# Fused attention and Fourier mixing with a feed-forward network: weight sums formed in the first feed-forward block, feed-forward PSUM split by accumulator, block sums on GpSimd

## The chip, the cores and the metric

The kernel runs on one core of one Trainium2 chip. The metric is the device time of one execution in microseconds. The core has a matrix engine (TensorE, PE in the profile, with PEld for its weight loads), two elementwise engines that can read the matrix engine's accumulators (VectorE or DVE, ScalarE or ACT), a general engine that can't (GpSimd or POOL), and SyncE (SP), which here only issues DMAs. Each engine works through its own instructions strictly in the order that was fixed at build time; between engines, semaphores make an instruction wait for its data or for a buffer to come free. PSUM, the accumulator memory, has eight banks of 512 floats per partition.

## The reference, cut to what matters

```python
# q, k, v: (8, 12, 448, 64); w_pre, w_post: (12, 12)
scores = scale * np.matmul(q, k.transpose(0, 1, 3, 2))
scores = np.einsum('bhij,hg->bgij', scores, w_pre)
attn = softmax(scores)                       # max, exp, sum + 1e-9
attn = np.einsum('bhij,hg->bgij', attn, w_post)
x = np.matmul(attn, v) -> (8, 448, 768)

u = x + np.real(fft(fft(x, axis=1), axis=2))
un = (u - mean(u)) / np.sqrt(var(u) + 1e-06)
out = u + np.maximum(un @ w_ch1, 0.0) @ w_ch2   # (768, 3072), (3072, 768)
```

`w_ch1` and `w_ch2` come as 64-bit floats, everything else as 32-bit floats. The kernel computes in 32-bit floats.

## The kernel before, in words

**The mixing stage** (`mix_phase`) makes `u` and writes it to a scratch in device memory. The scores of ten query rows and all twelve heads stand as one tile of 120 rows. There are 360 such tiles; a loop at the end of the function takes one step for each, and in each step it emits one tile's gather (a DMA on SyncE, L248), pre-mix matmul (L254), row maximum (L261, VectorE), exponential (L270, ScalarE), reciprocal (L278 and L280, VectorE), scaling of the post-mix matrix (L283, GpSimd), flip matmul (L291) and copy out of PSUM. What is not done for every tile (loading and transposing q and k, L161 and L222; scores, L234; the products with v, L315; the Fourier steps, L345 and L369) lies in a list `fill` with due steps, and is emitted in order of those. The tile framework then orders the instructions of each engine by its own estimate of when they can run, within what the buffers allow; so an entry of the list may run well ahead of its step.

The weight conversion is such an entry too (`emit_convert`). There are 96 pieces of 128 x 384, 48 of each matrix, due every 3.5 steps. A piece is loaded as pairs of 32-bit words by a GpSimd DMA (L399, tag `raw64`, two buffers) and made into floats by seven VectorE instructions (L414 to L427). The feed-forward network multiplies 2 x 2 blocks of matrices by Strassen's scheme in Winograd's form, with seven products in place of eight. This needs four weight blocks and some sums of them. Four pieces, one of each block, fill slots of one buffer `wu` (pool `pwu`, one buffer); after the fourth, four GpSimd sums (L431) are formed in it, and the seven operands are stored by SyncE to the scratches `w1s` (L532, three DMAs) or `w2s` (L543).

**The feed-forward stage** (`ffn_phase`) takes 512 rows of `u` at a time, in 7 blocks. `norm` normalises 128 rows and transposes them into `ub`, and after the fourth forms the four input sums (L627). `first` multiplies by the first matrix: for each of six pairs of tiles `m` it runs the seven products in the order 0, 1, 4, 5, 2, 6, 3 for both tiles, in three accumulators for each tile. Accumulator P takes products 0, 5, 6 and 3 and is read out after each; Q takes 1; R takes 4 and 2. The read-outs are L651, L655, L657 (ScalarE copies), L653, L659, L661 (VectorE additions) and L663. The weights of one `m` are one DMA of seven operands (L589, three buffers). `second` multiplies by the second matrix in the same way, with its weights loaded by half an operand (L594, four buffers), and adds to `u` (L696). The normalising of the next block runs inside it. All accumulators and the transposes of `norm` take PSUM tiles of one tag with eight buffers (`ps_tile`).

Of the kernel before, what the change touches and what calls it, by code (L numbers as in the profile page):

```python
# [10 lines left out]
F32 = mybir.dt.float32  # L11
# [5 lines left out]
P = 128  # L17
# [104 lines left out]
def mix_phase(ctx, tc, ident, q, k, v, w_pre, w_post, u_scr, weights):  # L122
# [7 lines left out]

    praw = pool("praw", 2)
    pqt = pool("pqt", NHP)
# [9 lines left out]
    pcv = pool("pcv", 2)  # L142
    pwu = pool("pwu")
    cst = pool("cst")
# [249 lines left out]

    units = {}

    def emit_convert(key, slot, src, r0, c0, sums, store):
        raw = pcv.tile([P, WC, 2], U32, name="raw64", tag="raw64")
        nc.gpsimd.dma_start(  # L399
            out=raw.rearrange("p n w -> p (n w)"),  # L400
            in_=src[r0:r0 + P, c0:c0 + WC].bitcast(U32))

        def done():
            if key not in units:
                units[key] = [pwu.tile([P, 8, WC], F32, name="wu", tag="wu"), 0]
            wu = units[key][0]
            units[key][1] += 1
            lo, hi = raw[:, :, 0], raw[:, :, 1]
            top = wu[:, slot, :]
            tmp = pcv.tile([P, WC], F32, name="tmp", tag="tmp")  # L410
            topb, tmpb = top.bitcast(U32), tmp[:, :].bitcast(U32)


            nc.vector.tensor_scalar(tmpb, hi, 0x7fffffff, None, op0=ALU.bitwise_and)  # L414
# [3 lines left out]
            nc.vector.tensor_scalar(topb, tmpb, 0x07ffffff, 3, op0=ALU.bitwise_and,  # L418
                                    op1=ALU.logical_shift_left)
# [7 lines left out]
            nc.vector.tensor_tensor(top, top, tmp[:, :], op=ALU.add)  # L427
            ev.d += 7 * (60.0 + WC * 1.042)
            if units[key][1] == 4:
                for out, x, op, y in sums:  # L430
                    nc.gpsimd.tensor_tensor(wu[:, out, :], wu[:, x, :], wu[:, y, :],  # L431
                                            op=op)
                store(units.pop(key)[0])
        return 0, [done]
# [9 lines left out]
    for gn, g in enumerate(groups):  # L444
# [19 lines left out]
        if g["gi"] == NG - 1:  # L464
# [5 lines left out]
            for x in range(NG):  # L470
                due(f + n + 7.6 + x, lambda g=groups[gn - NG + 1 + x]: emit_s2(g))
    for x, cut in enumerate(weights(nc)):
        due(x * WSTEP, lambda cut=cut: emit_convert(*cut))
# [40 lines left out]


ORDER = (0, 1, 4, 5, 2, 6, 3)
# [4 lines left out]

def _pieces(nc, w_ch1, w_ch2, w1s, w2s):

    out = []

    s1 = [(4, 7, ALU.add, 3), (5, 4, ALU.subtract, 0),
          (6, 0, ALU.subtract, 7), (2, 1, ALU.subtract, 5)]
    for n in range(DFF // 2 // WC):
        for kc in range(NK):
            def store(wu, n=n, kc=kc):  # L530
                for j in range(WC // P):
                    nc.sync.dma_start(out=w1s[n * (WC // P) + j, :, :, kc, :],  # L532
                                      in_=wu[:, 0:7, j * P:(j + 1) * P])
            for i, j in ((0, 0), (0, 1), (1, 0), (1, 1)):
                slot = {(0, 0): 0, (0, 1): 1, (1, 0): 7, (1, 1): 3}[i, j]
                out.append((("w1", n, kc), slot, w_ch1, j * DH + kc * P,
                            i * (DFF // 2) + n * WC, s1, store))

    s2 = [(4, 7, ALU.subtract, 0), (5, 2, ALU.subtract, 4),
          (6, 2, ALU.subtract, 7), (3, 1, ALU.subtract, 5)]  # L540
    for kf in range(NM):
        def store(wu, kf=kf):
            nc.sync.dma_start(  # L543
                out=w2s[:, kf // NQ, :, kf % NQ, :].rearrange("m p d -> p m d"),
                in_=wu[:, 0:7, :])
        for i, j in ((0, 0), (0, 1), (1, 0), (1, 1)):
            slot = {(0, 0): 0, (0, 1): 7, (1, 0): 1, (1, 1): 2}[i, j]
            out.append((("w2", kf), slot, w_ch2, i * (DFF // 2) + kf * P,
                        j * DH, s2, store))
    return out  # L550


@with_exitstack
def ffn_phase(ctx, tc, ident, u_scr, w1s, w2s, out):

# [12 lines left out]
    pst = pool("pst", 4)  # L568
    pps = pool("pps", 8, space=bass.MemoryType.PSUM)

    NT2 = TB // P
    HT = TB // 2

    def ps_tile():
        return pps.tile([P, 512], F32, name="ps", tag="ps")

# [9 lines left out]

    def load_w1(m):
        w = pw1.tile([P, 7, NK, P], F32, name="w1t", tag="w1t")
        nc.sync.dma_start(out=w[:, :, :, :], in_=w1s[m])  # L589
        return w  # L590

    def load_w2(i, half):
        w = pw2.tile([P, NQ, DH], F32, name="w2t", tag="w2t")
        nc.sync.dma_start(out=w[:, :, :], in_=w2s[i, half])  # L594
        return w
# [4 lines left out]
    def norm(t, x):  # L600
# [15 lines left out]
        for y in range(2):  # L616
            ps = ps_tile()
            for c in range(NK):
                cc = NK * y + c
                nc.tensor.transpose(ps[:, c * P:(c + 1) * P],  # L620
                                    un[:, cc * P:(cc + 1) * P], ident[:, :])
            nc.scalar.copy(  # L622
                out=ub[:, UB[y, x // 2], :, (x % 2) * P:(x % 2 + 1) * P],
                in_=ps[:, :NK * P].rearrange("p (c n) -> p c n", n=P))
        if x == NT2 - 1:
            for o, a, b in ((4, 6, 0), (5, 2, 4), (6, 2, 6), (3, 1, 5)):
                nc.vector.tensor_tensor(ub[:, o], ub[:, a], ub[:, b], op=ALU.subtract)  # L627

    def first(t):
# [5 lines left out]
        for m0 in range(0, NM, 2):  # L635
            ms = range(m0, m0 + 2)
            w = {m: load_w1(m) for m in ms}
            ps = {}
            for i in ORDER:
                for m in ms:  # L640
                    key = {0: "P", 5: "P", 6: "P", 3: "P", 1: "Q"}.get(i, "R")
                    opens = i in (0, 1, 4)
                    if opens:
                        ps[key, m] = ps_tile()
                    p = ps[key, m][:, :HT]
# [26 lines left out]
    def second(t, h):  # L672
# [4 lines left out]
        for n, i in enumerate(ORDER):  # L677
            key = {0: "P", 5: "P", 6: "P", 3: "P", 1: "Q"}.get(i, "R")
            opens = i in (0, 1, 4)
            for half in range(2):  # L680
                w = load_w2(i, half)
                for x in range(NT2 // 2):
                    if opens and half == 0:
                        ps[key, x] = ps_tile()
                    p = ps[key, x][:, :DH]
# [35 lines left out]
def kernel(  # L721
# [17 lines left out]
    u_scr = scr.tile([B * S, DM], F32, name="u_scr")  # L739
    w1s = scr.tile([NM, P, 7, NK, P], F32, name="w1s")  # L740
    w2s = scr.tile([7, 2, P, NQ, DH], F32, name="w2s")
    mix_phase(tc, ident, q, k, v, w_pre, w_post, u_scr,
              lambda nc: _pieces(nc, moe_w_ch1, moe_w_ch2, w1s, w2s))
    ffn_phase(tc, ident, u_scr, w1s, w2s,
              out.rearrange("b s d -> (b s) d"))
# [31 lines left out]
```

## Time and profile before

| what | value |
|---|---|
| median of 3 runs | 3284.43 us (3263.74 to 3286.43) |
| the profiled execution | 3276.48 us |
| its span | 3274.6 us |
| TensorE busy | 3024.8 us (92%) |
| VectorE busy | 1147.3 us (35%) |
| ScalarE busy | 794.0 us (24%) |
| GpSimd busy | 572.9 us (17%) |
| DMA | 449.91 MB, mean 137 GB/s |

The span is what the profiler recorded of one execution; the execution's own time is 1.9 us longer. A share of busy time is an average over stages: the mixing stage ends at about 1650 us, and the feed-forward blocks take the rest. In a row of a group the columns are line, engine, operation, output and inputs, shapes and count, then the busy time and the mean ns of one, then the idle time of the engine before them with what ended it. In a row of waits they are the waiting engine and line, what it waited for, and the sum in us, the number and the longest. In a row of a table of stretches they are the stretch and its length, for each engine the busy time and the number of instructions, then the clock granted to TensorE, the DMA engines' busy share and GB/s. In a row of the timeline they are the start, the duration, the engine, the line and the operation, with the idle time before it in brackets.

### The profile page before, as it was taken

Reading aid. Unit: us, or ns where it says so; the run is one execution under the profiler, and the core shown is the slowest. Engines: PE = TensorE matmul, PEld = TensorE weight load, DVE = VectorE, ACT = ScalarE, POOL = GpSimd, SP = SyncE. Lnnn points to the kernel's source line nnn. Section 1 sums busy time; section 2 is a strip of 40 time slices with the busy share of each in tenths; the row PEclk is TensorE's granted clock in tenths of the full one; section 3 lists DMA queues with packets and bytes.
Section 4 is the critical chain, followed back from the end, with each engine's and each line's share of the span. In section 5 each row is a group of like instructions: output and inputs, shape, how many; then the busy total and the mean of one; then the engine's idle time right before and its main releaser. Section 6 shows DMA issues by size and latency. Waiting matters only on the chain.

```text
span 3274.6 us, 39030 instructions
## 1 busy us (share of the span) xinstructions
PE 3024.8 (92%) x14768; PEld 2142.8 (65%) x14768; DVE 1147.3 (35%) x2843; ACT 794.0 (24%) x1940; POOL 572.9 (17%) x937
## 2 busy tenths in 40 slices
PE   6878888888899999999999999999999999999998
PEld 3545655555666767666777676686686675776775
DVE  4655556556333333333432132132222222221220
ACT  3332342433445444444211010010010010110100
POOL 4343353453413223131200000000000000000000
PEclk8898799999999999999999999999999999999999
DMA  7565566665544444444534443434434434444422
GB/s 178 136 155 144 135 154 172 164 163 153 118 82 87 85 82 96 69 99 70 186 115 154 152 170 145 166 139 165 173 135 155 161 153 153 164 150 152 155 108 106
DMA packets 146576, 449.91 MB, mean 137 GB/s; under 512 B 14175, under 2 KB 100191, under 8 KB 123095
## 3 DMA queue, kind: packets, MB, share of 16 engines
q1 hardware_dynamic: 121847, 354.61, 37.3%
q0 software_dynamic: 24544, 92.82, 9.2%
q8 instruction: 118, 1.93, 0.2%
q14 instruction: 67, 0.55, 0.0%
HBM read 315.24 MB, written 55.05 MB: 113 GB/s over the span
## 4 chain that ended last, share of the span: by engine, by line
PE 49%; issue 29%; DMA 13%; DVE 5%; POOL 2%; ACT 1%; SPq 1%; POOLq 0%; DVEq 0%; ACTq 0%
PE ps L687 10%; PE ms L315 9%; PE ps L647 9%; PE fl L291 6%; DMA raw<-in_moe_w_ch_dram 6%; PE mx L254 5%; PE ms L369 3%; PE ms L234 3%; PE ms L345 2%; DMA w1s<-wu 2%; DMA rawk<-in_k_dram 2%; DMA out_dram<-u 1%; DMA u<-u_scr 1%; DVE nmx L261 1%; DMA w2s<-wu 1%
## 5 line engine op out<-in xcount | busy, mean ns | idle before, releaser
L647 PE MATMUL ps<-ub,w1t 128*128 128x256 f32 x3528 | 791.0, 384 | 50.8 <-DVE h L661 17.2
L647 PEld LDWEIGHTS ps<-ub,w1t 128*128 128x128 f32 x3528 | 669.6, 192 | 172.2 <-ACT h L651 30.2
L687 PE MATMUL ps<-w2t,h 128*128 128x384 f32 x2352 | 763.6, 486 | 0.0
L687 PEld LDWEIGHTS ps<-w2t,h 128*128 128x128 f32 x2352 | 445.0, 190 | 303.8
L291 PEld LDWEIGHTS fl<-kw2s,PP 120*112 120x112 f32 (+1 forms) x2880 | 350.4, 185 | 241.6 <-issue 117.2
L291 PE MATMUL fl<-kw2s,PP 120*112 120x120 f32 (+1 forms) x2880 | 392.3, 282 | 66.9 <-POOL kw2s L283 56.3
L254 PE MATMUL mx<-Kr,kw 120*120 120x448 f32 x720 | 350.7, 571 | 21.9 <-ACT PP L270 16.2
L270 ACT ACTIVATE PP<-mx,nmx 120x448 f32<-120x448 f32 x360 | 228.6, 635 | 526.9 <-DVE nmx L261 488.9
L315 PEld LDWEIGHTS ms<-vn,Pav 112*120 112x120 f32 (+1 forms) x3072 | 316.0, 182 | 21.3 <-issue 16.1
L315 PE MATMUL ms<-vn,Pav 112*120 112x64 f32 (+1 forms) x3072 | 315.4, 265 | 7.7 <-issue 6.9
L261 DVE TENSOR_REDUCE nmx<-mx 120x1 f32<-120x448 f32 x360 | 221.8, 616 | 221.9 <-PE mx L254 219.6
L283 POOL TENSOR_SCALAR kw2s<-kw2g,rcp 120x120 f32<-120x120 f32 x360 | 155.5, 432 | 691.1 <-DVE rcp L280 622.4
L707 POOL DMA_DIRECT2D out_dram<-u x7 | 5.6, 795 | 1484.7 <-DVE u L696 1484.7
L696 DVE TENSOR_TENSOR u<-u,ps 128x384 f32<-128x384 f32 x98 | 54.4, 555 | 551.9 <-PE ps L687 551.9
L104 ACT COPY Pav<-fl 112x480 f32<-112x480 f32 x310 | 177.0, 572 | 252.2 <-PE ms L315 131.9
L234 PE MATMUL ms<-kT,qT 64*120 64x448 f32 (+1 forms) x768 | 210.4, 619 | 9.3 <-DVE Sb L106 6.2
L104 ACT COPY Sb<-ms 120x448 f32<-120x448 f32 (+1 forms) x324 | 161.1, 531 | 50.9 <-PE ms L234 50.7
L653 DVE TENSOR_TENSOR h<-h,ps 128x256 f32<-128x256 f32 x84 | 35.4, 422 | 332.9 <-PE ps L647 332.9
L622 ACT COPY ub<-ps 128x384 f32<-128x384 f32 x56 | 24.0, 483 | 479.8 <-PE ps L620 479.7
L234 PEld LDWEIGHTS ms<-kT,qT 64*120 64x120 f32 (+1 forms) x768 | 57.4, 182 | 121.7 <-issue 73.8
L254 PEld LDWEIGHTS mx<-Kr,kw 120*120 120x120 f32 x720 | 109.5, 193 | 30.0 <-ACT PP L270 20.8
L278 DVE TENSOR_SCALAR rcp<-den 120x1 f32<-120x1 f32 x360 | 54.5, 152 | 211.0 <-ACT PP L270 206.0
(75 smaller groups left out, 2163.3 us busy)
## 6 DMA issues: line engine op xcount, KB each, us to landing
w1t<-w1s SPq DMA_DIRECT2D x84, 1344.0 KB
w2t<-w2s SPq DMA_DIRECT2D x98, 1152.0 KB
Kr<-Sb SPq DMA_DIRECT2D x352, 210.0 KB
raw<-in_moe_w_ch_dram POOLq DMA_DIRECT2D x96, 384.0 KB, 5.7
w1s<-wu SPq DMA_DIRECT2D x36, 448.0 KB
w2s<-wu SPq DMA_DIRECT2D x12, 1344.0 KB
rawq<-in_q_dram POOLq DMA_DIRECT2D x96, 112.0 KB, 6.0
rawk<-in_k_dram POOLq DMA_DIRECT2D x96, 112.0 KB, 5.8
```

The costliest lines, as they stand in the source:

```text
L104: self.nc.scalar.copy(out=out, in_=in_)
L234: nc.tensor.matmul(sp[:n, :S], st["qT", hp][x * D:(x + 1) * D, g["i0"]:g["i0"] + n], st["kT", hp][x * D:(x + 1) * D, :], start=True, stop= ...
L254: nc.tensor.matmul(mx[:m, :S], kw1[:m, :m], tiles[T]["Kr"][:m, :], start=True, stop=True)
L261: nc.vector.tensor_reduce(nmx[:m, :], tiles[T]["mx"][:m, :S], axis=AX.X, op=ALU.max, negate=True)
L270: nc.scalar.activation(PP[:m, :], tiles[T]["mx"][:m, :S], ACTF.Exp, bias=tiles[T]["nmx"][:m, :], accum_out=den[:m, :])
L283: nc.gpsimd.tensor_scalar(kw2s[:m, :], kw2g[:m, :], rcp[:m, :], 1.0, op0=ALU.mult, op1=ALU.mult)
L291: nc.tensor.matmul(fl[:PC, jc * KR:(jc + 1) * KR], tiles[T]["PP"][:m, jc * PC:(jc + 1) * PC], tiles[T]["kw2s"][:m, :], start=True, stop=True)
L315: nc.tensor.matmul(ps[:n, hl * D:(hl + 1) * D], g["Pav"][:, jc * NH + h, :n], st["v", h // 2][:, h % 2, jc * D:(jc + 1) * D], start=(jc == ...
L345: nc.tensor.matmul(ps[:w, :SH + 1], g["xf"][par][:n, d0:d0 + w], ts[:n, g["gi"], par, :], start=(g["gi"] == 0), stop=(g["gi"] == NG - 1))
L369: nc.tensor.matmul(ps[:n, :DH + 1], st["z", par, ch][:, i0:i0 + n], tab[:w, ch, :], start=(ch == 0), stop=(ch == len(chunks) - 1))
L647: nc.tensor.matmul(p, w[m][:, i, kc, :], ub[:, i, kc, :], start=opens and kc == 0, stop=kc == NK - 1, skip_group_check=True)
L687: nc.tensor.matmul(p, lhs[i][:, half * NQ + kf, x * P:(x + 1) * P], w[:, kf, :], start=opens and half == 0 and kf == 0, stop=half == 1 and ...
```

## The change

The mixing stage now only converts. Each piece has its own result tile `top` (two buffers) and is stored by itself, by one SyncE DMA, to new scratches `w1f` and `w2f` that hold the four blocks of each matrix. The buffer `wu`, the GpSimd sums and the stores of seven operands are gone, and the q and k loads have three buffers instead of two (`praw`).

The sums are formed in the first feed-forward block. For `t == 0`, `load_w1` loads the four blocks of an `m`, forms four sums on VectorE in the tile that TensorE will use, and stores them to `w1s`. A new function `sum_w2`, called for both tiles of each pair, does the same for one twelfth of the second matrix, in a buffer of the `pw2` pool, and stores to `w2s`. Later blocks load an `m` with four DMAs, from both scratches. `load_w2` takes blocks from `w2f` and sums from `w2s`.

The PSUM tiles have three tags: four buffers for P, two for Q (which `norm` uses too) and two for R. The input sums in `norm` go from VectorE to GpSimd.

```diff
-    praw = pool("praw", 2)
+    praw = pool("praw", 3)
...
-    pwu = pool("pwu")
...
+        top = pcv.tile([P, WC], F32, name="top", tag="top")
+        tmp = pcv.tile([P, WC], F32, name="tmp", tag="tmp")
...
-            if units[key][1] == 4:
-                for out, x, op, y in sums:
-                    nc.gpsimd.tensor_tensor(wu[:, out, :], wu[:, x, :], wu[:, y, :],
-                                            op=op)
-                store(units.pop(key)[0])
+            nc.sync.dma_start(
+                out=dst, in_=top.rearrange("p (m f) -> p m f", m=split))
...
+    def ps_tile(key):
+        return pps.tile([P, 512], F32, name="ps" + key, tag="ps" + key,
+                        bufs=4 if key == "P" else 2)
...
+    def load_w1(t, m):
         w = pw1.tile([P, 7, NK, P], F32, name="w1t", tag="w1t")
-        nc.sync.dma_start(out=w[:, :, :, :], in_=w1s[m])
+        nc.sync.dma_start(out=w[:, 0:2], in_=w1f[m, :, 0:2])
+        if t:
+            nc.sync.dma_start(out=w[:, 3], in_=w1f[m, :, 3])
+            nc.sync.dma_start(out=w[:, 2], in_=w1s[m, :, 0])
+            nc.sync.dma_start(out=w[:, 4:7], in_=w1s[m, :, 1:4])
+            return w
+        nc.sync.dma_start(out=w[:, 6], in_=w1f[m, :, 2])
+        nc.sync.dma_start(out=w[:, 3], in_=w1f[m, :, 3])
+        for o, a, op, b in ((4, 6, ALU.add, 3), (5, 4, ALU.subtract, 0),
+                            (6, 0, ALU.subtract, 6), (2, 1, ALU.subtract, 5)):
+            nc.vector.tensor_tensor(w[:, o], w[:, a], w[:, b], op=op)
+        nc.sync.dma_start(out=w1s[m, :, 0], in_=w[:, 2])
+        nc.sync.dma_start(out=w1s[m, :, 1:4], in_=w[:, 4:7])
         return w
+
+    def sum_w2(kf):
+        w = pw2.tile([P, NQ, DH], F32, name="w2t", tag="w2t")
+        at = kf // NQ, slice(None), kf % NQ
+        nc.sync.dma_start(
+            out=w[:, 0:4, :],
+            in_=w2f[:, at[0], :, at[2], :].rearrange("b p d -> p b d"))
+        for o, a, b in ((4, 1, 0), (5, 3, 4), (1, 3, 1), (2, 2, 5)):
+            nc.vector.tensor_tensor(w[:, o], w[:, a], w[:, b], op=ALU.subtract)
+        for o, n in ((1, 0), (4, 2)):
+            nc.sync.dma_start(
+                out=w2s[n:n + 2, at[0], :, at[2], :].rearrange("b p d -> p b d"),
+                in_=w[:, o:o + 2, :])
...
-            ps = ps_tile()
+            ps = ps_tile("Q")
...
-                nc.vector.tensor_tensor(ub[:, o], ub[:, a], ub[:, b], op=ALU.subtract)
+                nc.gpsimd.tensor_tensor(ub[:, o], ub[:, a], ub[:, b], op=ALU.subtract)
...
-            w = {m: load_w1(m) for m in ms}
+            w = {m: load_w1(t, m) for m in ms}
+            if t == 0:
+                for m in ms:
+                    sum_w2(m)
```

More of the change, by code (lines that the diff above doesn't have):

```diff
@@ L401, in emit_convert @@
             in_=src[r0:r0 + P, c0:c0 + WC].bitcast(U32))
+        lo, hi = raw[:, :, 0], raw[:, :, 1]
+        top = pcv.tile([P, WC], F32, name="top", tag="top")
+        tmp = pcv.tile([P, WC], F32, name="tmp", tag="tmp")
+        topb, tmpb = top[:, :].bitcast(U32), tmp[:, :].bitcast(U32)
         def done():
[L404 to L411, printed above, removed]
             nc.vector.tensor_scalar(tmpb, hi, 0x7fffffff, None, op0=ALU.bitwise_and)
```

67 lines of the change are left out of this document (29 added, 38 removed).

## The prediction, made before the changed kernel had run

> **What bounds the kernel now.** I read the page's 40 slices first, then a table of stretches cut where the picture changes.
>
> ```profile
> span 3274.6 us, 39030 instructions
> ...
> PE   6878888888899999999999999999999999999998
> ```
> ```profile
> core 0: us, PE busy (x) PEld busy (x) DVE busy (x) ACT busy (x) POOL busy (x), PEclk, DMA share, GB/s
> 30.00:835.00 805.00, 656.20 (x3654) 439.74 (x3654) 468.97 (x1273) 279.35 (x680) 332.59 (x490) 0.90 0.60 154
> 835.00:1600.00 765.00, 741.58 (x4752) 527.87 (x4752) 260.34 (x750) 350.43 (x842) 189.17 (x364) 0.98 0.45 89
> 1651.00:1769.00 118.00, 113.38 (x511) 95.97 (x510) 35.17 (x71) 18.34 (x49) 0.57 (x1) 1.00 0.33 124
> 1769.00:1878.00 109.00, 109.00 (x356) 65.18 (x355) 19.46 (x26) 3.44 (x8) 0.00 (x0) 1.00 0.44 159
> ```
>
> TensorE is the bound from 835 us to the end (741.6 of 765, and 113 of 118 in the first feed-forward block). It isn't before 835 us, where it is busy 656 of 805. That stretch is the one in which weights are converted beside the mixing. The same table for the row maxima alone (one L261 per mixing step) gives the price:
>
> ```profile
> 30.00:835.00 805.00, 97.45 (x159) 0.90 0.60 154
> 835.00:1600.00 765.00, 122.02 (x198) 0.98 0.45 89
> ```
>
> Without conversion a step takes 765/198 = 3.86 us. The 159 steps before would have taken 614 us and took 805: the conversion costs **191 us**. The groups and the waits say how.
>
> ```profile
> L431 POOL TENSOR_TENSOR wu<-wu 128x384 f32<-128x384 f32 x96 | 97.7, 1028 | 14.7 <-DVE wu L427 10.1 <-DVE rcp L278 2.8
> L427 DVE TENSOR_TENSOR wu<-wu,tmp 128x384 f32<-128x384 f32 x96 | 52.6, 554 | 0.6
> L414 DVE TENSOR_SCALAR tmp<-raw 128x384 uint32<-128x384 uint32 x96 | 39.6, 413 | 155.3 <-DMA raw<-in_moe_w_ch_dram 155.3
> ```
> ```profile
> DVE wu L418 <- DMA w1s<-wu: 68.1, 11, 9.5
> DVE wu L418 <- DMA w2s<-wu: 32.8, 9, 7.2
> PE ms L222 <- DMA rawq<-in_q_dram: 28.9, 14, 9.7
> PE ms L222 <- DMA rawk<-in_k_dram: 19.5, 11, 2.9
> PE ps L647 <- DVE h L661: 17.2, 5, 4.4
> PE ps L647 <- ACT h L651: 16.2, 35, 0.5
> PE ps L647 <- ACT h L657: 16.2, 35, 0.5
> ```
>
> VectorE runs in a fixed order. When a conversion instruction at its head waits, the row maxima and reciprocals behind it wait too, and TensorE after them. There are two such waits: 155.3 us for raw pieces (L414), and 68.1 + 32.8 = 100.9 us in 20 waits, 5.0 us each, for the one sum buffer `wu` to be stored (L418).
>
> **Mixing stage.** The seven VectorE conversions of each of 96 pieces stay. Gone are the 96 GpSimd sums (97.7 us beside other work) and the single buffer's turn every four pieces: four sums, a store, 5.0 us. In its place each piece has its own result buffer, two in rotation, and its own store. I price what is left from stretches that have no turn in them: pieces two apart, whose raw buffer is the same, starting at L414.
>
> ```profile
> 45.10 0.34 DVE L414 TENSOR_SCALAR tmp<-raw 128x384 uint32<-128x384 uint32 x1
> ...
> 64.58 0.36 DVE L414 TENSOR_SCALAR tmp<-raw 128x384 uint32<-128x384 uint32 x1 [2.87 <-DMA raw<-in_moe_w_ch_dram]
> ...
> 795.84 0.36 DVE L414 TENSOR_SCALAR tmp<-raw 128x384 uint32<-128x384 uint32 x1 [0.73 <-DMA raw<-in_moe_w_ch_dram]
> ...
> 809.19 0.36 DVE L414 TENSOR_SCALAR tmp<-raw 128x384 uint32<-128x384 uint32 x1 [2.53 <-DMA raw<-in_moe_w_ch_dram]
> ```
>
> These are the first and the last of 46 such cycles, counted through the timeline; they average 10.68 us, with 103 row maxima in all, 2.24 steps each. 48 cycles would then lose 48 x (10.68 - 2.24 x 3.86) = 98 us, so 93 us less than 191. But 96 stores now stand in SyncE's queue between the gathers, and nothing in this trace shows a second ring of two buffers beside the raw one. Its price lies between nothing (a store has the whole next piece, 5.3 us, to land) and 5.0 us per piece, as in the turn: 480 us. I take 0.25 us per piece, 24 us, near the lower end, because the turn's 5.0 us held four GpSimd sums and a store of seven blocks, and this store holds one. **Conversion: -70 us** (-93 + 24, rounded). At most all 191 go.
>
> The third raw buffer for q and k aims at the waits of L222, 48.4 us of idle TensorE. Bounds 0 and -48. Half of the batches lie before 835 us, where the price above has their waits in it, which leaves 24; and GpSimd must still issue each load. **I take -15 us.**
>
> **Feed-forward PSUM.** The two rows with 35 waits are 5 pair boundaries in 7 blocks: TensorE runs one tile's products 0, 5 and 6 in a row, each behind ScalarE's copy of the same bank.
>
> ```profile
> 1900.89 0.37 ACT L651 COPY h<-ps 128x256 f32<-128x256 f32 x1 [0.91 <-PE ps L647]
> 1901.31 1.56 PE L647 MATMUL ps<-ub,w1t 128*128 128x256 f32 x6 [0.46 <-ACT h L651]
> 1902.91 0.37 ACT L657 COPY h<-ps 128x256 f32<-128x256 f32 x1 [1.65 <-PE ps L647]
> ```
>
> With one common tag, accumulator Q of the pair's first tile comes after P of its second in the rotation, and that one waits for its weight tile. With three tags Q and R of the first tile are free, products 1 and 4 go in between, and each copy is covered by 6 matmuls or more. Bounds 0 and -32.4; **I take -25 us**, since the second tile's product 0 then comes sooner after its load. L661's 17.2 us stay: VectorE is held there by the next block's input.
>
> **Block sums on GpSimd.** Four sums of 768 columns move.
>
> ```profile
> L627 DVE TENSOR_TENSOR ub<-ub 128x768 f32<-128x768 f32 x28 | 25.6, 955 | 2.4 <-ACT ub L622 1.7
> L330 POOL TENSOR_TENSOR xe<-X 120x383 f32<-120x383 f32 x24 | 24.5, 1023 | 0.0
> L647 PE MATMUL ps<-ub,w1t 128*128 128x256 f32 x3528 | 791.0, 384 | 50.8 <-DVE h L661 17.2 <-ACT h L651 16.2 <-ACT h L657 16.2
> ```
>
> On VectorE 4 x 0.955 = 3.8 us; on GpSimd, twice L330's 1.023 for twice the columns, 8.2 us. For blocks 2 to 7 two of the seven products of the previous block still follow, about 31 us of its 109, so nothing. For the first block TensorE has products 0 and 1 before the first sum: 24 matmuls at 118 us/504, 5.6 us against 2.05; later sums come every 2 us against 2.8 per product. Zero; without cover, 4.4 us.
>
> **First block.** New there: 96 sums of 384 columns on VectorE (48 for each matrix), 96 x 0.554 = 53 us on top of 35 in 118 us: it fits. Of 24 tiles four blocks of 192 KB are read and four written.
>
> ```profile
> 1590.20 3.96 SPq L589 DMA_DIRECT2D w1t<-w1s  x3
> 1594.20 2.60 SPq L594 DMA_DIRECT2D w2t<-w2s  x4
> ```
> ```profile
> w1t<-w1s SPq DMA_DIRECT2D x84, 1344.0 KB
> ...
> raw<-in_moe_w_ch_dram POOLq DMA_DIRECT2D x96, 384.0 KB, 5.7
> ```
>
> A block is 1344/7 = 192 KB, so 24 x 8 x 196,608 B = 37.7 MB, against 14.6 (124 GB/s x 118). At full share the conversion stretch moves 154/0.60 = 257 GB/s, the first block 124/0.33 = 376, the later mixing 89/0.45 = 198: 147 us, 100 or 191. I take 147, since its rows are nearest in size. Seven of the 24 tiles can be fetched from 1590 us on, which leaves 104 in 118 us: it fits, barely. What doesn't hide is VectorE at a sum whose tile hasn't landed, with the evictions behind it. The nearest row is L414: 155.3/96 = 1.62 us per load. 17 x 1.62 = **+27 us**; bounds +5 and +74 (serial case below). In later blocks four loads per tile instead of one are 36 more issues of about 0.3 us on a queue with 118 us: nothing.
>
> **Sum:** -70 - 15 - 25 + 27 = -83. The profiled execution took 3276.5 us (span 3274.6 and 1.9 around it), so 3193.5. The runs' median, 3284.4, is 8 higher, their lowest 3263.7; I predict **3194 us**.
>
> **Rivals.**
> *The store ring decides (slower).* SyncE is held at gathers, and a store behind a held gather holds VectorE at L418.
>
> ```profile
> SPq L248 <- PE mx L254: 589.9, 183, 12.6
> ```
>
> That is 3.2 us a time. One such hold for every two pieces is 48 x 3.2 = 154 us in place of my 24: conversion +61, total +48, **3324 us**. It is slower than before from 24 + 83 = 107 us of store waits, 1.1 us per piece. Against: two pieces per buffer turn, 10.7 us, usually outlast a 3.2 us hold and a 5.7 us landing. Chance 0.09.
> *The conversion gains nothing:* the seven instructions and all raw waits remain, pieces only crowd closer. Total -13, **3263 us**, chance 0.16.
> *The first block goes serial:* SyncE holds each load behind the previous tile's store, which waits for its sums: 24 x (5.7 + 4 x 0.554) = 190 us against 118, +72. Total -38, **3238 us**, chance 0.12. For: SyncE's order is fixed. Against: at 1590 us seven loads leave the queue within 6.6 us, less than two landings of 5.7 us. The Trainium skill, "DMA: Bandwidth & Descriptors", section "Anatomy of one DMA", fits about 2.0 us fixed per DMA plus bytes at 436 GB/s; an estimate by it, were all 96 DMAs of this block serial, is 192 + 87 = 279 us, and the sum would come to +51. The trace disagrees that they go one by one, by the seven loads in 6.6 us.
> *More goes:* with the turn gone, raw waits halve too; 98 becomes 49, conversion -142, the total -155: **3121 us**, chance 0.10.
>
> **Numbers.** The forecast has 0.53. By itself it spans 3135 to 3245 (conversion -93 to -40, first block +5 to +50). The range 3115 to 3268 takes in the third and fourth rival and most of the second; it leaves out the store ring and tails. A measurement here tells about 1% from no change, 3252 to 3317. Faster by over that: 0.49 of the forecast's 0.53, 0.10, 0.08 of the serial case, 0.06 of the second rival: 0.73. Slower by over it: 0.08, and the rest 0.19.
>
> **What would show it.** Right: the stretch to the end of conversion is shorter, with fewer than 835 us and 5.3 us per piece; L418 waits for stores under 25 us; TensorE's waits at L651 and L657 gone; L222's under 30; the first block 118 to 170 us. Wrong: L418 waits above 107 us in all, L414 waits well above 155, or a first block near 190 with VectorE waiting at its sums.

## The result, and the profile after

The changed kernel takes 3174.91 us (median; 3171.81 to 3191.58) against 3284.85 (3263.74 to 3286.43) for the kernel before. The ratio is 0.9685, with a 95% interval of 0.9639 to 0.9731: faster by 3.2%. The forecast was 3194, with a range of 3115 to 3268.

The profiled execution of the changed kernel was the slowest of its four (3191.58, span 3189.8), so the accounts below are made span against span: 3274.6 before, 3189.8 after, 84.8 us less. By the medians it is 110 us less. First the page's span and slices after:

```profile
span 3189.8 us, 39781 instructions
...
PE   6888888899999999999999999999999999999998
```

Before, TensorE reached nines in the twelfth slice of 40, now in the ninth. The conversion stretch ends sooner. The tables of stretches for the row maxima say what that is worth. I cut them at the first and the last conversion instruction, and again at the last batch's first product with v. Before (row maxima at L261):

```profile
28.90:832.80 803.90, 96.83 (x158) 0.90 0.61 154
832.80:1518.80 686.00, 106.49 (x172) 0.98 0.44 87
```

After (row maxima at L260; the columns are stretch, length, VectorE's busy time on that line with its count, TensorE's granted clock, DMA share, GB/s):

```profile
25.60:619.80 594.20, 68.84 (x112) 0.84 0.65 161
619.80:1441.20 821.40, 135.00 (x219) 1.00 0.46 90
```

A step outside the conversion fell from 686.0/172 = 3.99 us to 821.4/219 = 3.75. The conversion's loss, worked out as in the prediction, is 803.9 - 158 x 3.99 = 174 us before and 594.2 - 112 x 3.75 = 174 us after. The stretch is shorter only because fewer steps lie in it: the 96 pieces are packed closer. The same mixing code, profiled in four of the runs below (the repeat, and the runs with one tag, without sums and with block sums on VectorE), loses 161 to 184 us, and that of the kernel before, profiled with the three tags, 186. So two losses are told apart only from about 25 us on. Over the 331 steps the lower step time makes 331 x 0.237 = 78 us, and the whole of mixing, to the last batch's products with v, is shorter by 1518.8 - 1441.2 = 77.6.

The rest of the account is in the tables of stretches over all engines. Before: the end of mixing up to the first feed-forward matmul, then the first block's first half, then everything from its second half on.

```profile
1518.80:1650.60 131.80, 128.42 (x868) 97.75 (x867) 58.13 (x168) 46.24 (x115) 25.22 (x52) 1.00 0.51 145
1650.60:1766.70 116.10, 111.48 (x507) 94.96 (x506) 35.41 (x73) 18.35 (x49) 0.80 (x2) 1.00 0.32 120
1766.70:3274.60 1507.90, 1452.86 (x5521) 1035.99 (x5519) 348.34 (x662) 129.16 (x337) 20.95 (x32) 0.99 0.41 151
```

The same after, with the conversion stretch ahead of them:

```profile
25.60:619.80 594.20, 493.08 (x2562) 336.38 (x2561) 404.12 (x1098) 195.56 (x475) 181.37 (x305) 0.84 0.65 161
619.80:1441.20 821.40, 821.36 (x5277) 582.91 (x5276) 290.62 (x837) 398.24 (x959) 215.67 (x415) 1.00 0.46 90
1441.20:1596.40 155.20, 140.30 (x859) 107.58 (x858) 79.16 (x210) 45.44 (x112) 27.95 (x51) 0.91 0.64 183
1596.40:1712.30 115.90, 111.10 (x516) 96.24 (x515) 58.42 (x122) 19.44 (x51) 8.70 (x6) 1.00 0.63 223
1712.30:3189.80 1477.50, 1441.88 (x5521) 1037.21 (x5519) 326.25 (x638) 129.56 (x337) 64.07 (x56) 0.99 0.44 155
```

| stretch | before | after | difference |
|---|---|---|---|
| to the last batch's first product with v | 1518.8 | 1441.2 | -77.6 |
| end of mixing, to the first feed-forward matmul | 131.8 | 155.2 | +23.4 |
| first half of the first block | 116.1 | 115.9 | -0.2 |
| all after that | 1507.9 | 1477.5 | -30.4 |
| span | 3274.6 | 3189.8 | -84.8 |

The sum is the -83 of the prediction almost to the microsecond, but its terms are not, and the closeness hangs on which execution was profiled (110 us by the medians). The waits after (engine and line, what it waited for, then the sum in us, the number, the longest):

```profile
DVE tmp L407 <- DMA raw<-in_moe_w_ch_dram: 121.7, 55, 5.6
...
DVE top L411 <- DMA w1f<-top: 15.8, 11, 3.3
PE psP L660 <- DMA w1t<-w1f: 12.7, 30, 2.6
PE ms L221 <- DMA rawq<-in_q_dram: 9.4, 1, 9.4
...
DVE top L411 <- DMA w2f<-top: 1.0, 3, 0.6
```

The store waits are 16.8 us where they were 100.9, and those for q and k 9.4 where they were 48.4. The raw waits stay (121.7 for 155.3) although there is less time for them to lie in. TensorE's 70 stops behind ScalarE's copies are gone; small waits for weight tiles stand in their place.

Where the +23.4 comes from is in the timeline after, on VectorE. Two of the first sums, with the idle time before each in brackets:

```profile
1503.47 0.56 DVE L582 TENSOR_TENSOR w1t<-w1t 128x384 f32<-128x384 f32 x1 [3.81 <-DMA w1t<-w1f]
...
1531.70 0.56 DVE L594 TENSOR_TENSOR w2t<-w2t 128x384 f32<-128x384 f32 x1 [8.96 <-DMA w2t<-w2f]
```

The first block's loads and sums do not begin with the block at 1596 us. They begin ahead of 1503 us, beside the last mixing steps, where VectorE waits for tiles with row maxima and evictions behind the waiting sum. Its waits for these tiles (L582 and L594) sum to 32.4 us, in 11.

### The profile page after: what moved, and what is told of

Read it like the earlier page. It is cut to its first block, busy times and chain, and to the rows that moved or that the text cites. A ratio compares the mean times of both kernels' runs of the same rounds, so it can differ in the third digit from the quotient of the medians.

```text
span 3189.8 us, 39781 instructions
## 1 busy us (share of the span) xinstructions
PE 3019.4 (95%) x14768; PEld 2167.1 (68%) x14768; DVE 1162.7 (36%) x2911; ACT 792.9 (25%) x1940; POOL 519.8 (16%) x869
## 4 chain that ended last, share of the span: by engine, by line
PE 66%; DMA 14%; issue 12%; DVE 5%; POOL 2%; SPq 1%; ACT 0%; POOLq 0%; DVEq 0%; ACTq 0%
PE ms L314 9%; PE psP L660 8%; PE fl L290 8%; PE psP L700 8%; PE mx L253 7%; DMA raw<-in_moe_w_ch_dram 6%; PE psR L700 6%; PE psR L660 5%; PE ms L233 4%; PE ms L368 4%; PE psQ L700 3%; DMA w1t<-w1f 3%; PE ms L344 2%; PE psQ L660 2%; DMA out_dram<-u 1%
## 5 line engine op out<-in xcount | busy, mean ns | idle before, releaser
L660 PE MATMUL psP<-ub,w1t 128*128 128x256 f32 x2016 | 465.8, 384 | 30.8 <-DVE mv L619 16.7
L660 PEld LDWEIGHTS psP<-ub,w1t 128*128 128x128 f32 x2016 | 383.7, 192 | 98.0 <-DMA w1t<-w1f 25.8
L700 PE MATMUL psP<-w2t,h 128*128 128x384 f32 x1344 | 436.9, 486 | 0.0
L700 PEld LDWEIGHTS psP<-w2t,h 128*128 128x128 f32 x1344 | 254.8, 190 | 173.1
L260 DVE TENSOR_REDUCE nmx<-mx 120x1 f32<-120x448 f32 x360 | 222.3, 618 | 256.4 <-PE mx L253 254.3
L660 PE MATMUL psR<-ub,w1t 128*128 128x256 f32 x1008 | 232.7, 380 | 0.9 <-DMA w1t<-w1s 0.7
L700 PE MATMUL psR<-w2t,h 128*128 128x384 f32 x672 | 220.0, 486 | 0.0
L637 POOL TENSOR_TENSOR ub<-ub 128x768 f32<-128x768 f32 x28 | 50.5, 1825 | 1038.2 <-ACT ub L632 1037.7
L660 PEld LDWEIGHTS psR<-ub,w1t 128*128 128x128 f32 x1008 | 191.3, 190 | 28.2 <-DMA w1t<-w1s 2.6
L700 PEld LDWEIGHTS psR<-w2t,h 128*128 128x128 f32 x672 | 126.4, 190 | 84.1
L709 DVE TENSOR_TENSOR u<-u,psP 128x384 f32<-128x384 f32 x56 | 31.1, 555 | 341.6 <-PE psP L700 341.6
```

Of the source, the lines that this page charges most:

```text
L260: nc.vector.tensor_reduce(nmx[:m, :], tiles[T]["mx"][:m, :S], axis=AX.X, op=ALU.max, negate=True)
L660: nc.tensor.matmul(p, w[m][:, i, kc, :], ub[:, i, kc, :], start=opens and kc == 0, stop=kc == NK - 1, skip_group_check=True)
L700: nc.tensor.matmul(p, lhs[i][:, half * NQ + kf, x * P:(x + 1) * P], w[:, kf, :], start=opens and half == 0 and kf == 0, stop=half == 1 and ...
```

## The experiments

Each ratio is to the kernel before on the same chip, with its 95% interval. The changed kernel itself, run again without an edit, gives the scale for differences:

> The changed kernel again, unchanged, as the comparison for the runs beside it: about 0.9685 of the kernel before, so 3165 to 3175 us.

It took 3185.41 us, ratio 0.9718 (0.9666 to 0.977), with single runs from 3166.78 to 3206.77; the median is above the 3165 to 3175 expected. So two variants of the changed kernel are told apart from about 1% on, and less is said below with care.

**Two buffers for q and k.**

```diff
-    praw = pool("praw", 3)
+    praw = pool("praw", 2)
```

> The changed kernel with two q and k buffers again instead of three. Theory A (read from the trace of after: mixing steps after conversion took 3.75 us instead of 3.95): the third buffer is worth about 45 us, so this runs in about 3220 us, TensorE waits for q and k again for about 45 us in all, and a batch takes about 178 us instead of 169. Theory B (the prediction's terms): it is worth 15 us, so about 3190 us, and a batch stays near 169 to 172 us.

It took 3217.94 us, ratio 0.983 (0.9798 to 0.9861), 1.1 to 1.5% above the changed kernel's two ratios, about 40 us. The row maxima and the waits:

```profile
28.20:604.00 575.80, 68.67 (x112) 0.86 0.67 165
604.00:1466.80 862.80, 134.98 (x219) 0.98 0.44 86
```
```profile
PE ms L221 <- DMA rawq<-in_q_dram: 19.4, 7, 9.6
...
PE ms L221 <- DMA rawk<-in_k_dram: 16.9, 12, 3.0
```

A step after the conversion takes 862.8/219 = 3.94 us, near the old 3.99, and 36.3 us of q and k waits are back. The conversion's loss is 575.8 - 112 x 3.94 = 135 us, 39 below that of both kernels and 26 below the lowest of the profiles counted above. So with two buffers the conversion probably did lose less than before, as far as one profile can say; the third buffer brings the steps down by 0.19 us each (63 us in 331) and the loss back up by 39. Its net is 1466.8 - 1441.2 = 26 us between these two profiles.

**One PSUM tag.** The rest of the change stays; the accumulators rotate through eight buffers of one tag again.

```diff
-        return pps.tile([P, 512], F32, name="ps" + key, tag="ps" + key,
-                        bufs=4 if key == "P" else 2)
+        return pps.tile([P, 512], F32, name="ps", tag="ps", bufs=8)
```

> The changed kernel with one common PSUM tag of eight buffers in the feed-forward stage again. Theory A: the three tags are worth about 35 us (5.1 us in each of 7 blocks), so this runs in about 3210 us with the two ScalarE-copy waits of 0.46 us at each of 35 pair boundaries back. Theory B (predicted): 25 us, about 3200 us. Rival C: the weight loads set those boundaries, and the tags only rename the wait: at most 10 us, 3185 us or less.

It took 3194.13 us, ratio 0.9762 (0.9725 to 0.9799), and the stretch from the first block's second half on took 1491.3 us, 13.8 more than after. The old stops hardly returned:

```profile
PE ps L659 <- DMA w1t<-w1f: 23.2, 31, 1.2
...
PE ps L659 <- ACT h L663: 0.9, 2, 0.5
```

With four loads to a tile, TensorE waits for a tile's later parts just where it used to wait for the copies. The loads hide what the single tag costs, so this run undercounts the tags. (In five other profiles with the four loads and the three tags, that stretch took 1476.3 to 1480.6 us.)

**The tags alone, in the kernel before.**

```diff
-    pps = pool("pps", 8, space=bass.MemoryType.PSUM)
+    pps = pool("pps", space=bass.MemoryType.PSUM)
...
-    def ps_tile():
-        return pps.tile([P, 512], F32, name="ps", tag="ps")
+    def ps_tile(key):
+        return pps.tile([P, 512], F32, name="ps" + key, tag="ps" + key,
+                        bufs=4 if key == "P" else 2)
```

> The kernel before with only the three PSUM tags. In the run with one tag the later six blocks were 13.8 us longer than in the changed kernel, of 30.4 us between the kernels. Theory A2: the tags give about half (14 to 16 us over seven blocks, 0.995 of before) and the split of the weight load into four gives the rest, so ScalarE-copy waits of 0.46 us vanish but TensorE waits for the whole 1344 KB load instead. Rival C: with one large load per tile the tags give nothing, within 5 us of before. Rival A: they give all 35 us alone, 0.989 of before.

It took 3236.24 us, ratio 0.9865 (0.9835 to 0.9895). In the table of stretches, the first block's first half and the rest:

```profile
1659.30:1769.70 110.40, 110.35 (x516) 96.27 (x515) 36.80 (x75) 19.43 (x51) 1.51 (x2) 1.00 0.34 128
1769.70:3237.60 1467.90, 1439.08 (x5521) 1038.82 (x5519) 347.56 (x662) 129.57 (x337) 20.91 (x32) 0.99 0.42 155
```

Against 116.1 and 1507.9 that is 45.7 us, for 70 stops whose idle time was 32.4. If all of it is theirs, a stop costs 0.65 us, 0.19 more than it stood idle. The timelines bear that price out at the boundary shown in the prediction: from 1896.70 us to the next group at 1901.31, eighteen matmuls took 4.61 us, and the six from there to 1903.34 took 2.03. In the run with the tags, eighteen behind the same wait for the next block's input took 3.99 and six took 1.30. The two stops cost 0.62 and 0.73 us there. TensorE's busy time fell as well, from 1452.86 to 1439.08 for the same 5521 matmuls. The changed kernel's later part is 9.6 us longer than this one (1477.5 against 1467.9); a run further down takes that up.

**No sums in the first block.** The rest of the change stays. Sums, their stores and the loads for the second matrix's sums are left out, and TensorE reads plain blocks in their place.

```diff
-        for o, a, op, b in ((4, 6, ALU.add, 3), (5, 4, ALU.subtract, 0),
-                            (6, 0, ALU.subtract, 6), (2, 1, ALU.subtract, 5)):
-            nc.vector.tensor_tensor(w[:, o], w[:, a], w[:, b], op=op)
-        nc.sync.dma_start(out=w1s[m, :, 0], in_=w[:, 2])
-        nc.sync.dma_start(out=w1s[m, :, 1:4], in_=w[:, 4:7])
+        nc.sync.dma_start(out=w[:, 2], in_=w1f[m, :, 0])
+        nc.sync.dma_start(out=w[:, 4:6], in_=w1f[m, :, 1:3])
...
-            if t == 0:
-                for m in ms:
-                    sum_w2(m)
```

> The changed kernel without any weight sums: the first block forms and stores none, its sum operands are loaded from the plain blocks, so its products are not the reference's; all loads of feed-forward operands stay in size. Theory A: the sums cost 28 us (23 of them in the end of the mixing stage, where they run early), so about 3147 us, and from the first product with v of the last batch to the first feed-forward matmul it takes about 131 us as in the kernel before instead of 155. Rival E: the sums hide, and the end of the mixing stage is slow for its own reasons: 3170 us or more.

It took 3159.9 us, ratio 0.965 (0.9612 to 0.9688). The same two stretches, end of mixing and first half of the first block:

```profile
1428.00:1561.10 133.10, 127.89 (x858) 96.87 (x857) 57.13 (x165) 45.26 (x112) 24.54 (x51) 1.00 0.53 142
1561.10:1673.90 112.80, 111.36 (x516) 96.14 (x515) 35.20 (x71) 19.44 (x51) 9.04 (x6) 1.00 0.37 125
```

Against 155.2 and 115.9 that is 22.1 and 3.1 us less: by the profiles the sums, with those transfers, cost 25 us, nearly all of it in the end of mixing, where the clock is 1.00 again in place of 0.91. By the medians it is 15 us (against 3174.91) to 26 (against 3185.41), somewhat less than the 28 of Theory A.

**Block sums back on VectorE.**

```diff
-                nc.gpsimd.tensor_tensor(ub[:, o], ub[:, a], ub[:, b], op=ALU.subtract)
+                nc.vector.tensor_tensor(ub[:, o], ub[:, a], ub[:, b], op=ALU.subtract)
```

> The changed kernel with the four input sums of each block on VectorE again. Predicted: they hide on either engine, so the same as the changed kernel, 0.965 to 0.975 of before. Rival J: on GpSimd they delay the first block or the block's output, then 5 to 10 us faster here; rival K: on VectorE they hold evictions, then 5 us or more slower here.

It took 3172.63 us, ratio 0.9683 (0.9653 to 0.9713): no difference. A sum takes 1825 ns on GpSimd and 955 on VectorE, and neither time shows. The group after:

```profile
L637 POOL TENSOR_TENSOR ub<-ub 128x768 f32<-128x768 f32 x28 | 50.5, 1825 | 1038.2 <-ACT ub L632 1037.7
```

**A third raw buffer.** If the conversion loses its time to raw waits, another buffer should save them.

```diff
-        raw = pcv.tile([P, WC, 2], U32, name="raw64", tag="raw64")
+        raw = pcv.tile([P, WC, 2], U32, name="raw64", tag="raw64", bufs=3)
```

> The changed kernel with three raw buffers for conversion pieces instead of two. Theory A: the conversion's loss of about 175 us comes from the ring of two raw buffers; with three, VectorE's waits for raw pieces fall from 122 us to under 40 and the run takes about 3125 us. Rival D: pieces are put closer together until something else holds them (SyncE at their stores, VectorE's own time), the loss per piece stays near 1.8 us, and the run takes 3165 to 3185 us, with the conversion ending earlier than 620 us.

It took 3176.78 us, ratio 0.9704 (0.9675 to 0.9733): no difference.

```profile
DVE top L411 <- DMA w1f<-top: 67.4, 24, 9.3
DVE top L411 <- DMA w2f<-top: 49.3, 21, 4.6
...
DVE tmp L407 <- DMA raw<-in_moe_w_ch_dram: 21.1, 16, 2.6
```

The raw waits fell from 121.7 to 21.1 us, and the waits for a result to be stored rose from 16.8 to 116.7. The sum is 138 in either case. The pieces came sooner to the next full ring: the stretch ends at 558.4 us in place of 619.8, with 102 steps in 532.5 us, and at the 3.785 us of a later step it still loses 146 us.

**One instruction in place of seven.** A piece is only masked, not converted.

```diff
-            nc.vector.tensor_scalar(tmpb, hi, 0x7fffffff, None, op0=ALU.bitwise_and)
...
-            nc.vector.tensor_tensor(top[:, :], top[:, :], tmp[:, :], op=ALU.add)
+            nc.vector.tensor_scalar(topb, hi, 0x3fffffff, None, op0=ALU.bitwise_and)
```

> The changed kernel with one VectorE instruction per conversion piece instead of seven (a mask of the high words, so the weights are not the reference's); loads and stores are kept. Theory G (the loss of about 174 us is VectorE's conversion work standing in front of the mixing's own): the loss falls to a seventh, 25 us, and the run takes about 3025 us. Theory F (the loss is VectorE held at pieces that were put too close to their loads and stores): pieces crowd closer, the conversion ends before 520 us, VectorE still waits over 100 us for raw pieces and results, and the run takes 3090 us or more.

It took 3144.89 us, ratio 0.96 (0.9566 to 0.9634). The row maxima, and the waits:

```profile
27.00:392.20 365.20, 37.51 (x61) 0.84 0.79 216
392.20:1394.80 1002.60, 166.74 (x269) 1.00 0.45 90
```
```profile
DVE top L407 <- DMA raw<-in_moe_w_ch_dram: 149.1, 66, 6.1
...
DVE top L407 <- DMA w2f<-top: 34.8, 12, 7.1
...
DVE top L407 <- DMA w1f<-top: 18.0, 7, 8.1
```

With six sevenths of the instructions gone, the stretch shrinks to 365 us and still loses 365.2 - 61 x 3.73 = 138 us. VectorE now waits 202 us in it. So the work is at most a small part of what the conversion costs: of 174 us, 36 went with it. Most of what is taken off a piece only brings the next one sooner, and that one waits.

**Pacing the pieces.** If crowding is the cause, then the whole work spread over all of mixing should cost next to nothing. The due steps in the list of entries don't hold a piece back, so a tiny GpSimd copy does: it reads the row maxima of a tile two steps ahead and writes into the buffer that the load, or the conversion, is going to fill. A load can then not start before its step, and a conversion not before three steps later.

```diff
-    def emit_convert(src, r0, c0, dst, split):
+    def emit_fetch(x, src, r0, c0, dst, split):
...
+        nc.gpsimd.tensor_copy(out=raw[:96, 0, 0:1].bitcast(F32),
+                              in_=tiles[now[0] + 2]["nmx"][:96, :])
...
+    def emit_convert(x, src, r0, c0, dst, split):
...
+        nc.gpsimd.tensor_copy(out=tmp[:96, 0:1], in_=tiles[now[0] + 2]["nmx"][:96, :])
...
-        due(x * WSTEP, lambda cut=cut: emit_convert(*cut))
+        due(1 + x * WSTEP, lambda x=x, cut=cut: emit_fetch(x, *cut))
+        due(4 + x * WSTEP, lambda x=x, cut=cut: emit_convert(x, *cut))
```

> The changed kernel with the pieces held to their due pace of 3.5 mixing steps: before each load and, three steps later, before each conversion a tiny GpSimd copy of the current step's row maximum is written into the piece's buffer, so neither can run ahead. Same result. Theory F (crowding): with a piece's load 11 us ahead and only one piece per 3.5 steps, VectorE waits for raw pieces fall from 122 us to under 30, the conversion lasts to about 1350 us, its loss falls from about 174 us to under 80, and the run takes 3060 to 3090 us. Theory G (work): the seven instructions cost the same wherever they stand, and the run takes 3150 us or more.

It took 3049.32 us, ratio 0.9316 (0.928 to 0.9352). The conversion stretch in the table over all engines, and the waits in it:

```profile
50.70:1329.00 1278.30, 1252.84 (x7981) 880.20 (x7979) 688.99 (x1944) 599.58 (x1453) 430.26 (x906) 1.00 0.58 130
```
```profile
DVE tmp L417 <- DMA raw<-in_moe_w_ch_dram: 41.8, 23, 4.4
DVE tmp L417 <- POOL tmp L412: 40.1, 62, 3.5
```

The stretch holds 337 steps of 3.79 us. At 3.75 they would take 1264 us, so the loss is 14 us in place of 174, with the same 96 loads, conversions and stores, and with 192 more instructions on GpSimd. TensorE is busy 98% of it at a clock of 1.00. Theory G is out. Theory F's time was too high, though VectorE's waits for raw pieces, 41.8 us, stayed above its 30, with 40.1 more at the new gate: spread out, such waits hardly reach TensorE. Counted through the timelines, TensorE idles 25.5 us in this stretch and only once for over 2 us (2.11); in the changed kernel's stretch it idles 101 us, 21 times for over 2 us, up to 6.71.

**One load for a weight tile**, as an edit of the paced kernel. The sums go back into the scratch of the blocks, which gets eight slots, so that a later block's `m` is one DMA of 1344 KB again in place of four.

```diff
         if t:
-            nc.sync.dma_start(out=w[:, 3], in_=w1f[m, :, 3])
-            nc.sync.dma_start(out=w[:, 2], in_=w1s[m, :, 0])
-            nc.sync.dma_start(out=w[:, 4:7], in_=w1s[m, :, 1:4])
+            nc.sync.dma_start(out=w[:, :], in_=w1f[m, :, 0:7])
             return w
```

> The paced kernel with one scratch of eight blocks for the first matrix, so that blocks 2 to 7 load a tile with one DMA of 1344 KB instead of four, and nothing else moves. Theory L (four small loads per tile cost the later blocks about 10 us: 1477.5 us from the first second product to the end in the changed kernel against 1467.9 with tags and one load): about 1468 us there and 3040 us in all. Rival: the difference lies elsewhere, and both stay at about 1477 and 3049.

The paced kernel's later part, and then this one's:

```profile
1562.00:3040.90 1478.90, 1441.75 (x5521) 1035.92 (x5519) 326.32 (x638) 129.56 (x337) 64.09 (x56) 0.99 0.44 154
```
```profile
1564.60:3035.00 1470.40, 1440.58 (x5521) 1040.92 (x5519) 325.78 (x638) 129.58 (x337) 64.08 (x56) 0.99 0.42 155
```

8.5 us came back, most of the 9.6, and twice the 4.3 us by which that part differs between the profiles with four loads. The whole took 3038.01 us, ratio 0.9278 (0.9251 to 0.9305), the lowest time of the study.

**Pacing with the sums still beside the mixing.** The same gates in the kernel with the three tags alone: sums on GpSimd in mixing, one sum buffer, two buffers for q and k.

```diff
-        due(x * WSTEP, lambda cut=cut: emit_convert(*cut))
+        due(1 + x * WSTEP, lambda x=x, cut=cut: emit_fetch(x, *cut))
+        due(4 + x * WSTEP, lambda x=x, cut=cut: emit_convert(x, *cut))
```

> The kernel before with the three PSUM tags (0.9865 of before by themselves) and the pieces held to their due pace in the same way; sums in the mixing stage, one sum buffer, two q and k buffers. Theory H (what costs is pieces crowding; the sum buffer's turn is only one form of it): paced, VectorE waits for the buffer's stores fall from 101 us to under 20, the conversion's loss from about 174 us to about 60, and the run takes about 3120 us; the rest down to 3049 is the third q and k buffer less the sums of the first block. Rival I (the single sum buffer is a cost of its own that needed removing): VectorE still waits 60 us or more for its stores, the run takes 3180 us or more.

It took 3123.98 us, ratio 0.9537 (0.9499 to 0.9575).

```profile
54.60:1436.90 1382.30, 207.21 (x336) 0.96 0.56 131
```
```profile
DVE wu L428 <- DMA w1s<-wu: 34.6, 6, 7.1
...
PE ms L222 <- DMA rawk<-in_k_dram: 29.2, 15, 3.5
...
PE ms L222 <- DMA rawq<-in_q_dram: 19.8, 9, 9.4
...
DVE wu L428 <- DMA w2s<-wu: 4.9, 2, 4.4
```

At 3.99 us for each of the 336 steps the loss is 42 us where it was 174. VectorE still waits 39.5 us for the one sum buffer, which lies between Theory H's 20 and Rival I's 60; the time is Theory H's. The 49 us of q and k waits stand in the steps. Pacing alone is worth 0.9537/0.9865, 3.3%; on top of it, the rest of the change, with the sums in the first block and the small loads paid, is worth 3123.98 - 3049.32 = 75 us, between two chips (72 by the ratios).

**A third buffer for the rows of u**, since TensorE still waits in the fastest kernel for a later block's input to be normalised:

```diff
-    pu = pool("pu", 2)
+    pu = pool("pu", 3)
```

> The kernel of the run beside it with three instead of two buffers for the 512 input rows, so that a block's rows are loaded before the block before has stored its output. Theory: the wait of TensorE behind VectorE's normalising at the start of five blocks (16 to 18 us in all) goes, so about 17 us less than the run beside it, near 3023 us. Rival: the buffer takes room that the first weight loads used early, the start of the first block is later by as much, and nothing is gained.

It took 3050.58 us, ratio 0.9315 (0.929 to 0.934), not better than without it (0.9278). The waits without it, and with it:

```profile
PE psP L670 <- DVE mv L629: 18.1, 5, 5.1
```
```profile
PE psP L670 <- DVE mv L629: 14.7, 4, 5.0
...
PE psP L670 <- DVE rstd L631: 6.4, 1, 6.4
```

Nothing went: 18.1 became 21.1 with the reciprocal's wait. The first feed-forward matmul came later, at 1460.4 in place of 1446.3 us, as the rival had it. What holds the normalising, when it isn't the buffer, stays open.

No run has three buffers for q and k in the kernel before; the third buffer was only taken out of the changed one.

## Why the prediction was right, and where it was not

**The total** was right by luck, through two errors that cancel. Mixing was to give 70 + 15 = 85 us, and gave 77.6, with nothing from the term that was to give most of it. (The forecast's span also starts too low: by its own terms, -93 - 15 - 25 + 5, it begins at 3149 us, not at 3135.)

**Conversion, -70.** This step failed. Between the two kernels the loss is 174 us both times. The single buffer's turn did go, as the prediction said, and the store ring did not take its place: 16.8 us of store waits, where 24 were assumed. What failed is the price of what is left, which I took from pairs of pieces that had no turn in them: 10.68 us for two pieces and 2.24 steps. Now two pieces take 594.2/48 = 12.4 us, and 112/48 = 2.33 steps pass; one piece takes 6.2 us, where under 5.3 was to be the sign of being right. Why those stretches were faster stays open. That they had found their raw data fetched ahead, while VectorE stood in a turn, is not borne out: summed over the timelines, VectorE waits 2.4 us for raw data in one of the 46 cycles and 2.5 us for two pieces now. What does differ in the profile is TensorE's granted clock, 0.91 to 0.94 over those cycles and 0.84 now. "Pieces only crowd closer" was my second rival, and for the mechanism it was the right one; the time came out otherwise since other terms were larger. The run with two q and k buffers (135 us of loss) suggests, as far as one profile can, that a part of the gain, 39 us, was there and was spent again once q and k were fetched earlier. Whether those loads take it through the DMA engines or through GpSimd's queue isn't separated.

**Why a crowded stretch loses.** In it TensorE did its 2562 matmuls in 493.08 us of 594.2, at a granted clock of 0.84. Taken shape by shape, the same matmuls would be 16% shorter at the means of the later stretch, about 413 us. So some 101 us of the stretch are idle and some 80 are slower matmuls, 181 in all, against 174 by steps. The timeline after shows both at one wait, on VectorE and then on TensorE:

```profile
127.76 0.36 DVE L407 TENSOR_SCALAR tmp<-raw 128x384 uint32<-128x384 uint32 x1 [2.02 <-DMA raw<-in_moe_w_ch_dram]
...
128.51 0.62 DVE L260 TENSOR_REDUCE nmx<-mx 120x1 f32<-120x448 f32 x1
...
129.37 0.16 DVE L279 RECIPROCAL rcp<-rcp 120x1 f32<-120x1 f32 x1
```
```profile
130.13 1.87 PE L290 MATMUL fl<-kw2s,PP 120*112 120x120 f32 x8 [2.37 <-POOL kw2s L282]
131.80 1.70 PE L253 MATMUL mx<-Kr,kw 120*120 120x448 f32 x2
...
134.44 1.07 PE L290 MATMUL fl<-kw2s,PP 120*112 120x120 f32 x8
135.35 0.92 PE L253 MATMUL mx<-Kr,kw 120*120 120x448 f32 x2
```

VectorE waits for a raw piece; the row maximum and the reciprocal behind it come late, GpSimd scales its matrix late, and TensorE idles for 2.37 us. The same instructions then take 1.87 and 1.70 us, and some 4 us later 1.07 and 0.92. The Trainium skill, "TensorE: Matmul & The Clock Gate", section "Part 1: The HAM clock gate", says that the clock is halved by default and after an idle window of about 3.4 us, and full again after about as long of work. This trace agrees on the halving and on the way back, but 2.37 us of idling were enough here. Slower transfers for TensorE itself are no rival: its own waits for a DMA sum to 2.6 us in the stretch, 1.2 of them for gathers. The paced kernel gives the other side: the same work without such gaps, a clock of 1.00 and 14 us of loss.

**Third buffer for q and k, -15.** Right in kind, mis-sized: 26 us between two profiles, about 40 by the medians. I halved its bound of 48 because half of the batches lie in the conversion stretch, but only 15.1 of the 48.4 us of waits lay there, and I counted waits only. It acts through every step: 0.19 us each with the rest of the change in place. The bound itself held.

**Feed-forward PSUM, -25.** Right, and larger: 30.4 us from the first block's second half on in the changed kernel, and 45.7 over all seven blocks by itself, above the bound of 32.4, because a stop costs more than its idle time. The waits at both copies are gone, as said. L661's 17.2 us stayed, as said, under another name: 16.7 us at VectorE's statistics for the next block's input (L619). Some 9.6 us are given back by the small loads, which I had at nothing: 36 more issues for a block are free for the queue, but the last part of a tile comes later, and TensorE waits 9.0 us for them from the first block's second half on.

**First block, +27.** Right in size (25 us against the profile without the sums), wrong in place. I had the loads begin at 1590 us and the waits in the block. The order moved them ahead of the block, where VectorE's waits stand ahead of row maxima, and the block itself was unchanged at 115.9 us. The serial case's 190 us did not come. (The 279 us beside it took, for this block's DMAs, which SyncE issues, a fit that the Trainium skill, "DMA: Bandwidth & Descriptors", section "Anatomy of one DMA", gives for DMAs issued by GpSimd.) The DMAs moved 223 GB/s in the block's 115.9 us, so at most 25.8 of the 37.7 MB lie in it and the rest before.

**Block sums on GpSimd, 0.** Right; 1.825 us each for an expected 2.05, and no difference in the run without.

**The rivals.** The store ring did not decide, with 16.8 us against the 107 at which it would. It does when the raw ring gets deeper (116.7 us), and even then the total stays, since the waits only change their place. "More goes, since raw waits halve" was wrong for the kernel as changed; the paced kernel is where they went, to 41.8 us, and the total passed below that rival's 3121.

**Still open:** how the paced kernel's gain divides between spreading the pieces and loading them three steps ahead, since the edit does both; and why the changed kernel's single runs spread by 40 us on one chip. The profiled ones spend 594 and 604 us in their conversion stretches for the same 112 steps, so at least a part lies there.

## What to carry to other kernels

Work that is hoisted into an in-order engine's stream runs as early as its buffers let it, and then its waits become everyone's waits. Giving it another buffer, or making it cheaper, mostly brings the next piece sooner: here 100 us of waits moved from one ring to another, and a seventh of the work still lost 138 us. Holding it back to an even pace took 160 of 174 us away. And before an accumulator rotation is left with one tag, look at which accumulator stands behind which: a 0.46 us wait, 70 times, cost 46 us.

## What the runs showed that I had not expected

A wait's idle time was not its price. A 0.46 us stop of TensorE cost 0.65 us, and in the conversion stretch the slower matmuls (some 80 us) cost nearly as much as the idling that came with them (101). A kernel with more instructions and the same DMA traffic was 4% faster than the changed one (3049.32 against 3174.91 and 3185.41) and TensorE had no idle time above 2.11 us in its conversion stretch. And splitting a 1344 KB load in four cost a total of 8.5 us over 72 tiles, 0.12 us each: little, but not nothing.
